# A second gradient accumulator, third buffers for YT and h_in, a warm SiLU, SEL cleared by GpSimd, and a new step order

## The chip, the cores and the metric

The kernel runs on one core of a Trainium2 chip. A core has five engines that each take their instructions in order: PE (TensorE, the matrix array), DVE (VectorE), ACT (ScalarE), POOL (GpSimd) and SP (SyncE, which here only issues DMAs). They meet through semaphores. SBUF is the on-chip memory (128 partitions), PSUM the accumulators that PE writes, DRAM what lies outside. The metric is the device time of one execution in microseconds; the median of three runs before the change is 574.38 us (573.65 to 574.65).

## The reference

One block of a network, forward and backward: layer norm, then a state-space convolution (S4) times a gate that is the SiLU of a two-layer feed-forward net, plus the input. The kernel returns the output and the gradients of eleven inputs.

```python
def _fwd_reference(A_u, ..., B_w1, B_w2):          # L = 2048 rows, D = 512, N = 128 states, F = 1792
    def _A_ref(u, A_re, A_im, B_re, B_im, C_re, C_im, log_dt, Dskip):
        dt = jnp.exp(log_dt)[:, None]
        P = jnp.exp((dt * (A_re + 1j * A_im))[:, :, None] * l[None, None, :])
        K = jnp.einsum("dn,dnl,dn->dl", Cc, P, dt * Bc).real        # the convolution kernel
        ...                                                         # causal convolution of u with K, by FFT
        return y + u * Dskip
    def _B_ref(x, w1, w2):
        return einsum(_silu(einsum(x, w1)), w2)
    xn = _layernorm(A_u)
    return A_u + _A_ref(xn, ...) * _silu(_B_ref(xn, B_w1, B_w2))

def reference(...):
    _out, _vjp = jax.vjp(_f, A_u, A_A_re, ..., B_w1, B_w2)
    return (_out, *_vjp(grad_out))
```

## The kernel before

The work is cut into some thirty streams. Each stream is a Python generator that emits a few instructions and yields; one such piece is a step. Nothing reorders the steps at run time: the string `PLAN`, cut by `/` into seven stages, names one stream per letter, and `play` takes the next step of that stream. So the string fixes the order of instructions on every engine and every queue. Two more strings go with it. `WAYS` says for each copy out of PSUM (through `k.ev`, line 113 or 114) whether ACT (`A`) or DVE (`D`) does it. `SLOTS` says which buffer each tile takes.

The stages, with the streams that matter below:

- Stage 0, the start. `1` loads the rows of x (SP) and log_dt (ACT queue); `0` loads the weights W1 and W2 (SP); `p` loads the S4 parameters by transposing DMAs (SP, line 363); `2` and `3` make constants and masks, `SEL` among them (lines 242 to 263, DVE and POOL); `4` makes the FFT tables `TF` with Sin on ACT (line 281); `5` makes smaller tables, with Sin at lines 314 and 315; `6` is the layer norm (statistics at line 375 and `xn` at 383 on DVE, the power `rstd` at 379 on POOL); `7` takes Exp of log_dt (506), forms `lamr` (508, DVE) and then 31 exponentials `mag_all` (511, ACT); `J` transposes rows of xn into XT on PE; `F` is the feed-forward net: `ps_h` on PE (755), a copy to `hT`, SiLU into `aT` (763), a store of hT to DRAM (765), then `ps_o` (772).
- Stage 1 and 2. `P`, `Q` and `R` build the convolution kernel on DVE, ACT and PE (`ps_k`, line 643), with round trips through DRAM (`ds<-Md`, `Ed`, `Yd`, `Kb`); `X` and `C` are the FFTs of input and kernel and their product; `F` goes on.
- Stage 3. The backward convolutions (`B`, `D`), and the backward feed-forward products `A` (1160) and `x` (1184).
- Stages 4 and 5. The gradients of the S4 parameters in four blocks of 128 channels: `N` folds the kernel gradient, `Y` loads the turned powers YT for sixteen groups (transposing DMAs, line 986; every fourth group is loaded plain as Yn and turned on PE), `V` multiplies (`ps_v`, 1012), `T` forms products on DVE (1029 to 1033), `S` sums them on PE (`psS`, 1049), and `Z` ends each block (lines 1067 to 1119). Beside them run the weight gradients: `h` loads rows of h (`h_in`, 1203), `t` turns them and takes SiLU (`a_tok`), `w` multiplies (1223); `g` loads `dh_tok` by transposing DMAs (1238) and `v` multiplies (1252).
- Stage 6. The rest of `v` and `w`, and the backward layer norm `i`, `k`, `m`.

A step of `Z` in one block: several DVE products; the accumulator `g_acc` is written at line 1094 and added to at 1099 and 1100; `gout` is written at 1089 and 1098; PE transposes `gout` (`pt_g`, 1104), ACT copies it back, POOL stores it in six DMAs (1111); PE reduces `g_acc` over the partitions (`pd`, 1114), DVE writes the result into the first row of `g_acc` (1117), and POOL stores that (1119). Before the change `g_acc` and `gout` have one buffer each.

Of the kernel before, what the change touches and what calls it, by code (L numbers as in the profile page):

```python
# [18 lines left out]
P = 128  # L19
# [26 lines left out]
""".replace("\n", "").split("/")


SLOTS = dict(x.split("=") for x in """
fp.XT=01010101;pf.pf=012010021021021021021010120120120120120120120120120210210210201201201202102102102021021021021021201  # L50
201201201201021012102102102102102102020120210210202102102021021201201212102102102102102102010101201201202010202102120102
0120120120120210210210201;fp.hT=0101010101010101;fp.ob=0101010;dft.w8=21301203120132032103213032013021;pc.pc=01010110101
010010101010010101010101010101010101010101010101010101010010101010101010101010110101010101010101010101010101010101010101
010101010101010101010101010101010101001011010101010101010101010101010101010101010101010101011110101010101010110010101010
101010101010101;tbl.tv=01011101110101011101001011101010;tbl.ts=01010101010111010010101000101101;tbl.W=010101101011010110
10;dft.t4=010100101010;gate.g=01237456;gate.S=01;da.doT=01010101;dftb.w8b=1010;da.dhT8=20120120;go.go_s=01010101;da.dhT6
=10101010;go.go_r=010101;go.go_g=01010101;da.pd_s=101010101010;go.go_x=01201201;sb.YT=0101010101010101;sb.Eb=10101010;sb
.Gb=01010101;sb.Vb=1010101010101010;sb.Tp=0101010101010101;sb.Sa=0101;fw.h_in=01010101010101;fw.a_tok=01010101010101;fw.
o11=01201201201201;fw.dh_tok=2012012;fw.o10=0101010;lw.pd_l=012301;lw.Gt=20132013;lw.m=010101;lw.o1=12031203
""".replace("\n", "").split(";") if x)  # L60

WAYS = """J=DAADADAA;
F=AAADAAAAADDADAAAAAAAAAAAAAAAAAAAAAAAAAAADAAAADDAAAAAAAAADDDADAAAADDDDAAA;
X=AAAAAAAAAAAAAAAAAAAAAAAAAAAAAAAA;
U=AD;
R=DDAADAAAAAAAAAAAAAADAAAADADDDAAAAAAAADDAAAAAAAAA;
C=DDDAAAAAAAAAAAAAAAAADDAAAAAAAADAAAAAADADDAADADAAADADDDADAAAAAAAA;
W=DDDDDDDDDDDDDD;  # L70
D=AAAADDAAAAAAAAADAAADAAAAAADAAAAAAADAAAAA;
d=DDDDDAAA;
B=AAAAAAAAAAAAAADAAAAAAAAAAAAAAADAAAAADADAAAAAADAAAAAADAAD;
x=AAADDAADAAAA;
V=AAADADAADAADAAAADDDAAAAAAAAAAAAAAAADADAAAAAAAAAAAAAAAAAAAAAAAAAA;
Y=DAAAADAA;
w=AAADAAAAADAAAD;
v=AADDADADAAAAAAADDAAAAAAAAAAA"""


class Placed:
# [79 lines left out]
def setup_tiles(k, wp):  # L161

    D = k.D
    t = SimpleNamespace()
    def new(nm, shape, dt=F32, pool=wp):
        setattr(t, nm, pool.tile([P] + shape, dt, name=nm))
    for nm in ("ldt", "Ar", "Ai"):
        new(nm, [D], BF16)
    new("lamr", [D])
    new("ph", [D])  # L170
    new("MS", [4, 128], BF16)
    new("il", [16], I32)
# [17 lines left out]
    new("m4", [4])  # L190
    new("rl", [NE])
# [45 lines left out]
def gen_masks(k, w):  # L237

    nc, const = k.nc, k.const
    G = nc.gpsimd  # L240
    MS, FO, SEL = w.MS, k.FO, k.SEL
    nc.vector.memset(MS[:], 0.0)
    nc.vector.memset(FO[:], 0.0)
    nc.vector.memset(SEL[:], 0.0)
    yield
    I = k.ident
    par = lambda t: t.rearrange("p (r b a) -> p r b a", b=2, a=4)
# [19 lines left out]
def gen_tables(k, w):  # L267
# [4 lines left out]
    def twiddles(h):  # L272
# [8 lines left out]
        nc.scalar.activation(out=k.TF[:, hs], in_=low, func=ACT.Sin, scale=-2 * PI_LO / 2.0 ** PB)  # L281
        yield
    yield from twiddles(0)
# [775 lines left out]
def gen_ssm_grads(k, b, sb):  # L1059
# [408 lines left out]
```

## Time and profile before

The profiled execution took 573.83 us, of which 572.1 us lie between its first and last instruction (the span). All times below are counted from the start of the span.

| | busy us | share of the span |
|---|---|---|
| PE | 528.9 | 92% |
| DVE | 526.4 | 92% |
| ACT | 446.4 | 78% |
| POOL | 75.6 | 13% |
| mean granted TensorE clock | 0.984 | |

An instruction's row gives its start, its length, engine, line, operation and tiles (`out<-in`); in brackets stands how long its engine was idle before it and what it waited for. "PEq", "SPq" and so on are an engine's queue work: issuing DMAs, semaphores. A window row gives the busy time of each engine in a stretch, then the clock that the throttle granted to PE (1.00 is full speed) and the share of time in which the DMA engines were busy. The chain of waits is the chain of work that ended last, followed back from the end; it shows by how much each instruction pushes the next (its pitch), a little less than its length where two overlap.

### The profile page before, as it was taken

What the parts mean: (1) busy time and instruction counts of PE and PEld (TensorE: products, weight loads), DVE (VectorE), ACT (ScalarE), POOL (GpSimd) and SP (SyncE); (2) the same over time, 40 slices, a digit from 0 to 9 for tenths busy, and PEclk for the clock granted to TensorE, in tenths of its full rate; (3) what the DMA queues carried; (4) which work ended last, traced back from release to release, by engine and by line L of the source; (5) the groups of instructions that cost most, each with busy time, mean ns of one, the idle gap of its engine ahead of it and who ended that gap; (6) DMA issues with size and microseconds to landing.
All of it is one profiled execution on the core that took longest, in us unless ns stands there. A gap on an engine that the chain in (4) does not pass through costs nothing.

```text
span 572.1 us, 14533 instructions
## 1 busy us (share of the span) xinstructions
PE 528.9 (92%) x6008; PEld 395.0 (69%) x6008; DVE 526.4 (92%) x826; ACT 446.4 (78%) x553; POOL 75.6 (13%) x163
## 2 busy tenths in 40 slices
PE   0599998999898999999999999999999999989995
PEld 0366766686767685877686766777668797857674
DVE  8999999999999879999999899969999999977994
ACT  7989989999999859998888785674477676843662
POOL 5321101010100011000000000000000030324121
PEclk9879999999999999999999999999999999989998
DMA  9988897988989989878888979898999989989893
GB/s 236 319 307 173 252 283 227 341 254 227 306 260 261 299 292 337 286 258 237 288 282 276 301 234 299 231 222 190 278 222 231 203 254 198 270 161 221 244 229 131
DMA packets 156643, 144.75 MB, mean 253 GB/s; under 512 B 83488, under 2 KB 132896, under 8 KB 153504
## 3 DMA queue, kind: packets, MB, share of 16 engines
q1 hardware_dynamic: 146816, 121.00, 78.6%
q0 software_dynamic: 6640, 19.67, 10.2%
q10 hardware_dynamic: 3120, 3.15, 1.7%
q8 instruction: 47, 0.77, 0.6%
q14 instruction: 20, 0.16, 0.1%
HBM read 62.91 MB, written 59.38 MB: 214 GB/s over the span
## 4 chain that ended last, share of the span: by engine, by line
PE 58%; DVE 22%; DMA 9%; ACT 4%; SPq 3%; issue 3%; POOL 1%; DVEq 0%; ACTq 0%; POOLq 0%
PE ps_w L1252 7%; PE ps_da L1160 7%; PE ps_dx L1184 7%; PE ps_w L1223 6%; PE ps_o L772 4%; PE pt_t L135 4%; PE ps_i L444 3%; PE ps_i L457 3%; PE ps_h L755 3%; DMA ds<-Md 2%; PE ps_s L399 2%; PE ps_s L427 2%; PE pt_f L413 2%; PE psS L1049 2%; DVE ds L602 2%
## 5 line engine op out<-in xcount | busy, mean ns | idle before, releaser
L113 ACT CAST dA<-ps_s 128x1024 bf16<-128x1024 f32 x86 | 86.2, 1032 | 5.7 <-PE ps_s L399 3.7
L755 PE MATMUL ps_h<-XT,W 128*128 128x256 bf16 x448 | 61.1, 289 | 11.9 <-DVE XT L114 6.3
L755 PEld LDWEIGHTS <-W 128*128 128x128 bf16 x448 | 44.6, 103 | 21.3 <-issue 11.5
L113 ACT CAST Vb<-ps_v 128x672 bf16<-128x672 f32 x55 | 39.0, 731 | 24.5 <-PE ps_v L1012 13.1
L1160 PE MATMUL ps_da<-doT,W 128*128 128x256 bf16 x448 | 56.3, 273 | 0.0
L1252 PE MATMUL ps_w<-dh_tok,xn 128*128 128x256 bf16 x448 | 52.3, 273 | 0.0
L1223 PE MATMUL ps_w<-YD,a_tok 128*128 128x512 bf16 x224 | 52.3, 388 | 0.0
L113 ACT CAST dB<-ps_i 128x1024 bf16<-128x1024 f32 x40 | 40.9, 1044 | 14.2 <-PE ps_i L444 13.9
L772 PE MATMUL ps_o<-W,aT 128*128 128x512 bf16 x224 | 51.0, 379 | 0.1
L1184 PE MATMUL ps_dx<-W,dhT 128*128 128x512 bf16 x224 | 50.9, 379 | 0.0
L1160 PEld LDWEIGHTS <-W 128*128 128x128 bf16 x448 | 41.5, 98 | 8.2 <-issue 1.8
L1252 PEld LDWEIGHTS <-xn 128*128 128x128 bf16 x448 | 43.0, 98 | 5.6 <-issue 0.6
L1163 DVE TENSOR_TENSOR dhT<-ps_da,dhT 128x512 bf16<-128x512 f32 x56 | 37.8, 683 | 6.1 <-PE ps_da L1160 4.6
L1223 PEld LDWEIGHTS <-a_tok 128*128 128x128 bf16 x224 | 22.0, 100 | 24.5 <-issue 2.2
L772 PEld LDWEIGHTS <-aT 128*128 128x128 bf16 x224 | 21.0, 98 | 25.1 <-issue 1.2
L1184 PEld LDWEIGHTS <-dhT 128*128 128x128 bf16 x224 | 21.1, 98 | 24.8 <-issue 1.6
L1214 ACT ACTIVATE a_tok<-pt_t 128x1024 bf16<-128x1024 bf16 x28 | 28.7, 1036 | 4.6 <-PE pt_t L135 4.4
L574 ACT ACTIVATE sn<-V 128x2048 bf16<-128x2048 int16 (+1 forms) x16 | 30.4, 1899 | 0.2
L113 ACT CAST o<-ps_w 128x256 bf16<-128x256 f32 (+1 forms) x33 | 14.6, 451 | 19.6 <-PE ps_w L1252 13.1
L470 DVE TENSOR_TENSOR cm<-sp_in,dA 128x2048 bf16<-128x2048 bf16 x24 | 29.3, 1219 | 0.7
L472 DVE TENSOR_TENSOR sp_in<-sp_in,dA 128x2048 bf16<-128x2048 bf16 x24 | 29.3, 1220 | 0.6
L643 PE MATMUL ps_k<-W,YD 128*128 128x84 bf16 x512 | 25.2, 201 | 4.7 <-DVE ds L114 1.4
(239 smaller groups left out, 1246.0 us busy)
## 6 DMA issues: line engine op xcount, KB each, us to landing
Yd<-YD SPq DMA_DIRECT2D x8, 1024.0 KB, 5.2
sp_in<-Ud SPq DMA_DIRECT2D x8, 1024.0 KB, 9.1
h_in<-Hd SPq DMA_DIRECT2D x14, 512.0 KB, 5.6
Ed<-ds SPq DMA_DIRECT2D x8, 672.0 KB, 5.2
Eb<-Ed SPq DMA_DIRECT2D x8, 672.0 KB, 5.2
Hd<-hT POOLq DMA_DIRECT2D x8, 512.0 KB, 7.2
Ud<-dA SPq DMA_DIRECT2D x8, 512.0 KB, 6.4
KXd<-dA SPq DMA_DIRECT2D x4, 1024.0 KB, 5.6
```

The lines of the kernel that those rows point to most:

```text
L113: return self.nc.scalar.copy(out=out, in_=in_)
L470: TT(out=t2[:], in0=b[:, :, gs], in1=a[:, 1:2, gs].to_broadcast([P, 2, n, P]), op=ALU.mult)
L472: TT(out=b[:, :, gs], in0=b[:, :, gs], in1=a[:, 0:1, gs].to_broadcast([P, 2, n, P]), op=ALU.mult)
L574: nc.scalar.activation(out=sn[:, 0:n], in_=low, func=ACT.Sin, scale=-2 * PI_LO / 2.0 ** PB)
L755: nc.tensor.matmul(out=ps[:, j], lhsT=k.W1[:, dk, ft * P:ft * P + P], rhs=XTv[:, :, dk, :], start=(dk == 0), stop=(dk == DK - 1))
L772: nc.tensor.matmul(out=ps[:], lhsT=aT[:, ft, t * P:t * P + P], rhs=k.W2[:, ft, :], start=(ft == 0), stop=(ft == FT - 1))
L1160: nc.tensor.matmul(out=ps[:, j], lhsT=k.W2[:, ft, dk * P:dk * P + P], rhs=dTv[:, :, dk, :], start=(dk == 0), stop=(dk == DK - 1))
L1163: nc.vector.tensor_tensor(out=dh[:, i0:i0 + 2, :], in0=ps[:], in1=dh[:, i0:i0 + 2, :], op=ALU.mult)
L1184: nc.tensor.matmul(out=ps[:], lhsT=dhs[ft // 8][:, ft % 8, t * P:t * P + P], rhs=k.W1[:, :, ft * P:ft * P + P], start=(ft == 0), stop=(ft ...
L1214: yield from turned(k, lambda t: h[:, t], k.T, a, lambda out, in_: k.nc.scalar.activation(out=out, in_=in_, func=ACT.Silu))
L1223: nc.tensor.matmul(out=ps[:], lhsT=at[:, t, :], rhs=k.do[:, t, :], start=(t == 0), stop=(t == k.T - 1))
L1252: nc.tensor.matmul(out=ps[:], lhsT=k.xn[:, t, dk * P:dk * P + P], rhs=dh[:, t].rearrange("p j n -> p (j n)"), start=(t == 0), stop=(t == k ...
```

## The change

In the code, five places:

```diff
@@ gen_masks
     nc.vector.memset(MS[:], 0.0)
     nc.vector.memset(FO[:], 0.0)
-    nc.vector.memset(SEL[:], 0.0)
     yield
...
     G.tensor_copy(out=par(MS[:, 3])[:, :, 1], in_=par(MS[:, 1])[:, :, 1])
     yield
+    G.memset(SEL[:], 0.0)
+    yield
     for a in range(4):
         G.tensor_copy(out=lane(SEL[:, :, a])[:, :, :, a], in_=lane(MS[:])[:, :, :, a])
@@ gen_tables
         low = prod[:].bitcast(I16).rearrange("p t c (k w) -> p t c k w", w=2)[:, :, :, :, 0]
+        if h == 0:
+            nc.scalar.activation(out=w.warm[:], in_=k.onesf[:], func=ACT.Silu)
         nc.scalar.activation(out=k.TF[:, hs], in_=low, func=ACT.Sin, scale=-2 * PI_LO / 2.0 ** PB)
@@ gen_ssm_loads
-        YT = sb.tile([P, 2, 8, P], BF16, name="YT", tag="YT", bufs=2)
+        YT = sb.tile([P, 2, 8, P], BF16, name="YT", tag="YT", bufs=3)
@@ gen_ssm_grads
-    acc = tmp("acc", 1)
+    acc = sb.tile([P, 1, P], F32, name="g_acc", tag="g_acc", bufs=2)
@@ gen_dw2_loads
-        h = fw.tile([P, k.T, P], BF16, name="h_in", tag="h_in", bufs=2)
+        h = fw.tile([P, k.T, P], BF16, name="h_in", tag="h_in", bufs=3)
```

`warm` is a new tile of one element; nothing reads it. `PLAN`, `SLOTS` and `WAYS` are written anew. The first stage of `PLAN`:

```diff
-3212215p557536266767177p177667560077417767p73730757676J7J6F77077p7668475F73666676J778653601F773787F487F3J6F7FF74648FF5F6
-FFF6377F866JF7688F767476F8/
+221p32551512p5566073777171165553766767777J767774J6376777pF6767703076767884p6J7677777707F6067FJF86F46673F5F743FF776646FF6
+78F7366F883F7867F8FF86364/
```

Read letter by letter, this changes the order in the first stage as follows.

- SP issued x rows 0-1, Ar, x 2-3, Ai, x 4-7, W1 (two parts), x 8-11, Br, Bi, W1 (last part), W2, Cr, Ci, W2, x 12-15. It now issues Ar, x 0-1, x 2-3, Ai, W1 (first part), the other three x loads, Br, Bi, W1 (two parts), Cr, Ci, W2 (two parts).
- ACT took Exp of dt, the two Sin of lines 314 and 315, 23 exponentials, one copy of `ps_h`, the other eight exponentials, a copy of `ps_h`, Sin of TF's first half, a copy of XT, a copy of `ps_h`, SiLU, three copies, SiLU, Sin of TF's second half. It now takes the two Sin of lines 314 and 315, Exp of dt, all 31 exponentials, copies of `ps_h`, XT and `ps_h`, the warm SiLU, Sin of TF's first half, a copy, SiLU, three copies, SiLU, Sin of TF's second half.
- DVE makes the first small tables and the first product with the Sin tables (317) ahead of the first statistics, and `lamr` right behind the first two of them.
- On POOL the memset of SEL comes between the second and the third `rstd`.
- The PSUM slots of the first transposes and `ps_h` were 0,1,2,0,1,0,0,2,1; they are 0,1,2,0,1,2,0,2,1.

In the later stages every stream's own sequence is kept, and the letters are interleaved a little differently. Where the prediction touches them:

- `WAYS`: in stages 0 to 2, six copies of `ps_k` and three of `ps_h` go from DVE to ACT; three small copies into `KE`, and five of `ps_h` or `ps_o`, go from ACT to DVE; the FFT's exchange two each way. In stages 3 to 6 DVE hands some six copies more to ACT.
- `SLOTS`: YT rotates 2,0,1 instead of 0,1; h_in 0,1,2 instead of 0,1; g_acc 0,1,0,1.
- Block 2 of `Z`: DVE ran, from line 1117 of block 1 on, the product Tq of group 13, the first pair of `Z`, the group's difference Ts, then four steps of `Z` to the accumulator, Tp of group 14, and the last step. Now it runs 1117, Tq, Ts, four steps of `Z`, Tp, the accumulator's step, Tq of group 14, the last step. PE runs between `pd` of block 1 and the transpose of block 2: two transposes of h, psS 12, two `ps_v`, psS 13, a group of 1252, `ps_v`, a transpose of Yn, a group of 1252, two `ps_v`, a group of 1252, `ps_v`.
- SP in stage 5: the transposing loads of `dh_tok` for the third pair of row blocks stood ahead of Eb 12 and behind Yn of group 15; both now stand behind that Yn. h rows 12 are loaded in stage 5 instead of 6.

More of the change, by code (lines that the diff above doesn't have):

```diff
@@ new lines @@
+78F7366F883F7867F8FF86364/QXJFXPFFFJFPXFXXFX9XFXPFFPFXPPFFFFFFFFXUPFFQFJFFQRQQUQPFXQFXXQXPFQQXXRPQJPFRFPRFFPFXXFFRRFQFRF
+FFXXRRFFPFQXQQQRXFQXFUFFQRQRXJQXFFQRPRRQRXXRPRRQPRFFPFRRFXXFPUJRPRFFRQFPQRRXRQRRRQRQXFXFRQQCFQRXFXXQRRFXRPXFFFQRPFPPRQFP
+RCUCCCFCCFRRCCQRCFCRQCRFCXQQFCQFQXPCQQFXFQPCRCCQFFCFCCPRRFQXPRFFRXFRXFCCCRRFRXXXCFFFFQQQCRFRCQCFXRPQRCFRXQPCFCQRQRCQCRFQ
+CCQCRRRFRPFCXCPRRJFXXRXXPRFRXPUFFXCRJXRPPCRXQFCCXPXQFQQFQCCFFRCFCCQCQRQPFCFCFFQFQFFCRFQRFCFFCRJRCCCPCCRRCCFCRCRCCRCQCPRC
+QXQCFPXXXQFPRQCCRXXFCJFCCXQXRPCQRRQCRFFCQRQXFQCRFRXFRRFRPXXRPRFCXFRPCXFRRRFFFCXCXFCXFQRQRFFCCCCFRUCFJQCCCCRFFQQFQCRQCQCQ
@@ new lines @@
+RCRRCRCCRRCRRCRRRUCCCRQCRRRCRRRFCCCCRCJFCC/FCGFCFGGGGGCCCFCFFCFCGCGFCCCCCFFGCGFFMCFCCCGFGCFFGCGHCCGCGHCGHFWCCFCFGCCFGGCG
+CGCCGCFGCFCCFCCWCCWCWHWCWHHHCCWGDCLWWDCGHWWWCCCWDWWDCWDWWDDWWDGWWMWWDDDLDLMLWLDWMDMWDDDDD/DdDasEddDWadDEoDAsBAAAoABaDoAB
+AAAADoBADDBBAoBDBAoABDAAABDBsDAAAABBBADaADBBAABoBBBADDBBDBBlEBxBBDosABBAABOBABxaBEOBDxOolxoDlOABBxBdBBABODdDaOBxBOxsDOBo
+OODxoxBDoaoxBDlOBBAsBOABxBBOoADaaABDABBBOBDDBBABBABABDdABDEAAAdABBBBAAABosdoADODoABOBAdBOABoxDDABBABABOEoDABDBlOADDxsDDB
+AoxOADDOBoABxoDBAOABDsAoBBxODBdAxOAOBDABBAaaDBAAdBlDAoOBADAODBxxABOBDBxDDBDoBxBBBoxsoBxBDAEBBDOBBoABAsAaOAOxDABBxODxsBBa
@@ new lines @@
+BBBoxAABBBEABxsBBBOxBBABaABBAOOAOABBAaBAABBBBxBAABAAABddAxBBBBBBBAABBBBxABBABBA/ANNNYAANYNYNxVAxVsaVVdAxAYVVxdVVAVTAYYVA
+ATxVTVVYsxAAVVAAAxTsAVVTTVNASNTNxASAVTANVATAVVAVVAAVTNAYTVTxTYYTxTxYSYTTVAxTVYVSVVVVVVS/hTthVtTtYtVYVtVTtVtVStTVVThTwTVV
+TVSVVVTTwVTYwYYtVTtwSgVVVVSwTwtTTVtgYZYVwYTNZVVNTvSVhZTTYSNTYNVVvYVTgVvthVvVwVvVvSTtVtTVTVtVVZZYvVYSZTTVYwVSgtTVtZTwTZVt
+TVTVwVtSVTTTVVVSVTTTTwTwVvVVVvZNYZvTVZZNYVZNvNvZYYhthTvNttYtSVtvVZtwTtTZvTSZYYSVtwTTVhVYvSVVVVTVVZwYVwVVTtTwVYTtYhSVtvTV
+TTVwSVVtVTVVSSTVYYTTTVgVZwVVZTTZwwYgwTVZYvTVTttTZtYSVTSgVhTVSvZZVVZVvYYvwZZgtTvZTVVVZSTvVTVVTZTZVwZVvtTSvwwSTTZThtTTttZv
@@ L46 @@
+ZStSZhgttZZZvZZgvtvwwtgZZtwZwvvZvZZvhwv/itikhvkivvttkvkikvwvmtkvmwkvkkwmktmgktkivmvwkmktwmkgvwvikvvmmkkvmtkvvkktkmivvtkw
+mwgmkvkmikmwmkkkmmwkvmvkvvkvvvmvmvvmvvmm
 """.replace("\n", "").split("/")
 SLOTS = dict(x.split("=") for x in """
[L50 to L52 removed]
@@ L58 @@
-.Gb=01010101;sb.Vb=1010101010101010;sb.Tp=0101010101010101;sb.Sa=0101;fw.h_in=01010101010101;fw.a_tok=01010101010101;fw.
-o11=01201201201201;fw.dh_tok=2012012;fw.o10=0101010;lw.pd_l=012301;lw.Gt=20132013;lw.m=010101;lw.o1=12031203
+fp.XT=01010101;pf.pf=012012021021201212012021012012010120120120120120120120120120102102102101201201201012012012012012102
+102102102102012012012012012102101201212012012012012012012102102102102120120120120120121020121210101012010120120210210210
+2102012012102102020121021;fp.hT=0101010101010101;dft.w8=21301203121030230123012320312031;pc.pc=0101010101010001010101010
@@ new lines @@
+101010101010101010101010101010101001010101010101010101010101010101010101010101010101010101010101101010101010101010101010
+101010101010101010101010101010110101010101010101010101010101010101010101010101001010101010101010101010101010101010101010
+1;fp.ob=0101010;tbl.tv=01011101110101011010110101010101;tbl.ts=01010101010111010010101000101101;tbl.W=010101101011010110
+10;dft.t4=010011010101;gate.g=10237456;gate.S=01;da.doT=01010101;da.dhT8=20120120;dftb.w8b=1010;da.dhT6=10101010;go.go_s
+=01010101;go.go_r=010101;go.go_g=01010101;go.go_x=01201201;da.pd_s=010101010101;sb.YT=2012012012012012;sb.Eb=01010101;sb
@@ L60 @@
+.Gb=01010101;sb.Vb=0101010101010101;sb.Tp=0101010101010101;sb.Sa=1010;fw.h_in=01201201201201;fw.a_tok=10101010101010;fw.
+o11=01201201201201;sb.g_acc=0101;fw.dh_tok=0120120;fw.o10=1010101;lw.pd_l=012301;lw.Gt=01230123;lw.m=010101;lw.o1=120312
+03
 """.replace("\n", "").split(";") if x)
 WAYS = """J=DAADADAA;
-F=AAADAAAAADDADAAAAAAAAAAAAAAAAAAAAAAAAAAADAAAADDAAAAAAAAADDDADAAAADDDDAAA;
+F=AAADAAAAADADDAAAADADAAAAAAAAAAAAAAAAAAAAAAADADDAAAAAAAAADDDADAAADADDDAAA;
 X=AAAAAAAAAAAAAAAAAAAAAAAAAAAAAAAA;
@@ L67 @@
 U=AD;
-R=DDAADAAAAAAAAAAAAAADAAAADADDDAAAAAAAADDAAAAAAAAA;
-C=DDDAAAAAAAAAAAAAAAAADDAAAAAAAADAAAAAADADDAADADAAADADDDADAAAAAAAA;
+R=AAAAAAAAAAAAAAAAAAADAADDDAADAAAAAADAADAAAAAAAAAA;
+C=DDDAAAAAAAAAAAAAAAAADDAAAAAAAADAAAAAADAADAADDAADADADDDADAAAAAAAA;
 W=DDDDDDDDDDDDDD;
[L71 to L77, printed above, removed]
@@ L78 @@
-v=AADDADADAAAAAAADDAAAAAAAAAAA"""
+D=AAAADDAAAAAAAAADAAAAAADAAADAAAAAAADAAADA;
+d=DDAADAAA;
+B=AAAAAAAAAAAAAADAAAAAAAAAAAAAAAAAAAAAAADAAAADAAAAAAAADADA;
+x=AADAAAADADAA;
+V=DAADADDADAAAADAADDAAAAAAAAAAAAAAAAADAAAAAAAAAAAAAAAAAAAAAAAAAAAA;
+Y=AADDDAAA;
+w=AADAAAAAAADAAA;
+v=DAADAAAAAAADAAAAAAAAAAAAAAAA"""
 class Placed:
@@ L190, in setup_tiles @@
     new("m4", [4])
+    new("warm", [1])
     new("rl", [NE])
```

22 lines of the change are left out of this document (removed).

## The prediction

> **What bounds the kernel now.** I read first the windows by stage, then the waits, then the two places where TensorE (PE) stands still, instruction by instruction. The windows (columns: stretch, length, busy of PE, weight load, DVE, ACT, POOL, granted clock, DMA share, GB/s):
>
> ```profile
> 45.00:255.00 210.00, 198.77 (x2532) 150.47 (x2529) 199.75 (x260) 195.12 (x224) 20.59 (x28) 1.00 0.89 272
> 255.00:375.00 120.00, 119.65 (x1500) 86.97 (x1500) 112.52 (x146) 95.20 (x100) 6.48 (x12) 1.00 0.87 269
> 375.00:435.00 60.00, 58.20 (x564) 41.86 (x562) 54.81 (x81) 35.84 (x46) 1.10 (x2) 1.00 1.02 221
> 435.00:495.00 60.00, 60.00 (x674) 48.38 (x672) 58.55 (x94) 42.73 (x69) 11.61 (x21) 1.00 1.05 228
> 495.00:513.00 18.00, 15.38 (x151) 11.43 (x149) 14.33 (x29) 9.78 (x18) 3.74 (x7) 0.91 0.98 222
> 513.00:566.00 53.00, 52.57 (x444) 38.99 (x442) 45.73 (x116) 27.28 (x45) 14.80 (x26) 1.00 0.87 219
> ```
>
> From 45 us on PE is the rope: 119.65 of 120, 60.00 of 60 and 52.57 of 53 leave nothing to win there, since no matmul is added or removed. Time can come only from where PE is idle or slow: the start (before 45), 11.2 us of gaps in 45 to 255 where DVE (95%) and ACT (93%) are full too, 1.8 us in 375 to 435, and 2.6 us in 495 to 513. The last is one hole. DVE, POOL and PE around it (start, us, instruction, idle before it and its releaser):
>
> ```profile
> 492.30 0.27 DVE L1117 TENSOR_TENSOR g_acc<-pd,dt 1x128 bf16<-1x128 f32 x1
> ...
> 497.77 0.68 DVE L1089 TENSOR_TENSOR gout<-g_t,dt 128x512 bf16<-128x512 f32 x1
> ...
> 502.82 0.29 DVE L1094 TENSOR_TENSOR g_acc<-g_u 128x128 f32<-128x128 f32 x1 [3.49 <-DMA out_dram<-g_acc]
> ```
>
> ```profile
> 489.60 3.18 POOL L1111 DMA_DIRECT2D out_dram<-gout  x6 [10.73 <-ACT gout L1108]
> ...
> 494.06 0.52 POOL L1119 DMA_DIRECT2D out_dram<-g_acc  x1
> ```
>
> ```profile
> 504.81 0.51 PE L1104 MATMUL pt_g<-ident,gout 128*128 128x128 bf16 x6 [2.62 <-DVE gout L1098]
> ...
> 506.18 5.30 PE L1223 MATMUL ps_w<-YD,a_tok 128*128 128x512 bf16 x16
> ```
>
> An undisturbed group of the same sixteen matmuls, and the window behind the hole (granted clock third from the end):
>
> ```profile
> 454.35 3.62 PE L1223 MATMUL ps_w<-YD,a_tok 128*128 128x512 bf16 x16
> ```
>
> ```profile
> 506.00:508.00 2.00, 2.00 (x12) 0.88 (x9) 1.97 (x4) 2.00 (x5) 0.95 (x2) 0.54 0.46 72
> ```
>
> The single accumulator of block 1 is stored by a DMA issued at 494.06, behind six stores of `gout` on POOL's queue. Block 2 wants the same buffer at 499.3; DVE stands 3.49 us until the store has landed, and PE, whose next instruction needs DVE's `gout`, stands 2.62 us. Then the granted clock falls to 0.54, and the sixteen matmuls of L1223 take 5.30 us, where the group at 454.35 takes 3.62. So the hole costs 2.62 + 1.68 = 4.30 us.
>
> **Part 1: two accumulators.** Blocks 0 to 3 alternate, so block 2 takes the buffer of block 0, long stored. The 3.49 us go; what is late next? First, DVE's own work. Between the store's source (L1117) and the `gout` that PE needs the new order has one product more (Tq of the next group, 0.77); at the pitches of the chain of waits that stretch sums to 9.5 us. PE's work from the `pd` matmul ahead of L1117 to that transpose is 11.0 us in the new order: three groups of L1252 (1.75 each), two sums psS (1.17), three transposes (0.45), six short ps_v (0.29) and `pd`. DVE stands some 1.1 us behind PE there, so the two meet within half a microsecond. Second, `gout` has one buffer still:
>
> ```profile
> DMA to landing us min/median/max: 2.2/4.0/7.2
> ```
>
> Its last store was issued by 492.78 and lands, by this row, between 495.0 and 500.0, while block 2 writes `gout` at 497.77 without a wait. At the slow end that would be a new wait of 2.2 us. I take 0.4 us lost to both, so -3.9 us; bounds -1.0 (the `gout` store lands last, and the clock falls again) and -4.3.
>
> [...]
>
> **Part 2: the start.** ACT's first instructions, and its two lines with the later table loads (xcount: ns min/median/max, first and last start):
>
> ```profile
> 4.28 0.63 ACT L506 ACTIVATE dt<-ldt 128x512 bf16<-128x512 bf16 x1 [1.33 <-DMA ldt<-in_A_log_dt_dram]
> 4.93 1.28 ACT L314 ACT_TABLE_LOAD   x1
> 6.22 0.40 ACT L314 ACTIVATE sf<-kf,mpi 128x128 f32<-128x128 int32 x1
> 6.53 0.44 ACT L315 ACTIVATE sv<-kq,mpi 128x192 f32<-128x192 int32 x1
> 6.99 1.28 ACT L511 ACT_TABLE_LOAD   x1
> 8.28 12.06 ACT L511 ACTIVATE mag_all<-lamr 128x512 bf16<-128x512 f32 x23
> ```
>
> ```profile
> L281 ACT ACTIVATE TF<-prod x2: 1893/1902/1910, 26.8 to 36.6; 128x2048 bf16<-128x2048 int16 x2
> L281 ACT ACT_TABLE_LOAD  x1: 1283/1283/1283, 25.5 to 25.5; - x1
> ```
>
> ```profile
> 30.07 1.28 ACT L763 ACT_TABLE_LOAD   x1
> ```
>
> DVE, POOL, SP and PE in the same stretch, and the window of the low clock:
>
> ```profile
> 1.57 0.91 DVE L244 MEMSET SEL<- 128x1024 uint32 x1 [0.16 <-issue]
> ...
> 4.77 0.69 DVE L375 BATCH_NORM_STATS2 st<-x_sb 128x6 f32<-128x512 bf16 x1
> ```
>
> ```profile
> 17.96 1.39 POOL L379 TENSOR_TENSOR rstd<-ve,mhalf 128x4 f32<-128x4 f32 x1 [4.50 <-DVE ve L378]
> ```
>
> ```profile
> 1.20 1.24 SPq L363 DMA_TRANSPOSE Ar<-in_A_A_re_dram  x1
> ```
>
> ```profile
> 29.29 5.28 PE L755 MATMUL ps_h<-XT,W 128*128 128x256 bf16 x24 [1.93 <-DVE hT L114]
> 34.36 0.98 PE L135 MATMUL pt_t<-ident,xn 128*128 128x128 bf16 x8
> 35.18 3.18 PE L772 MATMUL ps_o<-W,aT 128*128 128x512 bf16 x14
> ```
>
> ```profile
> 25.00:35.00 10.00, 7.57 (x38) 5.37 (x38) 9.86 (x24) 9.57 (x10) 4.88 (x7) 0.50 0.93 351
> ```
>
> ACT is the full engine here: 23 of the 31 exponentials follow each other from 8.28 to 20.3, the other eight behind one evacuation. The second Sin of L281, at 36.6, has no load ahead of it although SiLU ran in between: SiLU's table holds Sin. With a one-element SiLU ahead of the first L281, the two loads at 25.5 and 30.07 become one: -1.28. The warm activation costs between nothing and the 0.40 of `sf`, 128 times its size; I take 0.3. The new order also puts Sin of L314 before Exp of dt, so of the three loads before 8.28 one goes, but nothing comes of it: the 31 exponentials wait for `lamr`, and DVE comes to `lamr` later. The SEL memset leaves DVE (-0.91), but Ar's transpose now stands first on SP and takes 1.24 us, so x arrives 1.2 to 1.3 us later, and the statistics that began at 4.77 begin near 5.7. Net zero to -0.3, and rstd of the first rows 1.7 us late, which the full ACT hides. On POOL the memset lies ahead of the third `rstd`; I price it at 0.91 (DVE's own row, with 4 bytes an element) to 1.82 (two bytes), and POOL has waited 4.50 us by then. Without that cover it would delay four rows of xn by as much.
>
> What PE gains is the clock. It is at half rate from 25 to 35 us, because it gets work only in pieces (7.57 of these 10 us, the last wait 1.93). In the new order all exponentials go before the first evacuation (16.3 us for 31 at the pitch of the 23, so near 24.6), then evacuations follow at short intervals, and the PSUM slots rotate 0,1,2,0,1,2: PE should run on from about 25.2 instead of 29.3, so the clock should come back some 3 us earlier, and the second SiLU, ahead of the second table Sin, ends near 35.3. The first output matmuls can then start near 34 instead of 35.18. I take -1.5 us; bounds -3.0 (clock and table in full) and +2.0 (late x passed on to PE, as the 1.7 us of rstd).
>
> **Part 3: evacuations and order, 45 to 255 us.** DVE loses six copies of `ps_k` and takes three small KE ones, and takes two more of `ps_h` or `ps_o`:
>
> ```profile
> 133.90 0.50 DVE L114 CAST ds<-ps_k 128x336 bf16<-128x336 f32 x1
> ```
>
> 6 x 0.50 less 3 x 0.25 (half a `ps_k` row) less 2 x 0.75 (by 512 elements against 336) is 0.75 us off DVE in 210. The rest is the same list in another order. I take -0.5; bounds -5.6 and +5.6, half of the 11.2 us of PE gaps either way, since nothing in the trace prices an order.
>
> **Part 4: third YT and h_in.**
>
> ```profile
> SPq L986 <- PE ps_v L1012: 7.3, 5, 2.5
> ```
>
> SP, which issues in order, stood 7.3 us for a free YT and no longer does. But PE has only 1.8 us of gaps in 375 to 435, and the DMA share is 1.02 to 1.05 there, so earlier issues only queue elsewhere. The moved transposes of `dh_tok` (both of the third pair now behind Yn of group 15) sum to the same SP time. -0.4; bounds -1.8 (all of the idle in 375 to 435) and +1.0 (an earlier h_in ahead of a needed YT, half a YT issue of the 2.5 us that one wait took). Evacuations moved off DVE after 255 lie under a full PE: zero; without that cover, some six of 0.7 us, the size of `ps_k` to YT copies. The last two stages' new step order: zero, PE is gapless to 565.6.
>
> **The sum.** -1.5 - 0.5 - 0.4 - 3.9 = -6.3 us. The profiled execution took 573.83 (span 572.1), 0.55 under the median of 574.38; so 567.5 there and 568.1 by the median. I say 568.0.
>
> **The rivals.** (a) *The wait only moves*: `gout`'s store takes the accumulator's place, the clock falls again; part 1 gives -1.0 and the total is 571. For it: same queue, same landing rows. Against it: `gout` of block 2 was written at 497.77 with no wait.
> (b) *The new order loses in the full stretch*: between 45 and 255 PE's gaps grow from 11.2 us because three full engines wait for each other in other places; DVE at 95% has nothing to catch up with. It decides from +5.8 us of gaps on (17 instead of 11.2). At seven tenths more (+8) the kernel takes 576.6, slower. For it: each step of the 600 was moved a little, and one wait of 2 us on DVE there would pass on in full. Against it: DVE and ACT both get lighter, and the sequence of SP is nearly the same.
> (c) *More comes*: the start's bound of -3.0 and 3 us of gaps saved, 564.
> (d) *The table count does not fall* (the warm SiLU gets a load of its own and the Sin another): the start gives 0, the total 569.5; this lies in the forecast's own range.
> (e) *The hole costs only its idle time*: had the low clock behind it another cause, which stays, the total would be 569.8. Against it: of the six stages quoted from 45 us on, only the one with the hole is under 1.00. [...]
>
> **How the numbers follow.** Forecast with (d) 0.61, own range 565 to 571; (a) 0.12; (b) 0.16; (c) 0.08; (e) 0.03. About 0.2% (1.15 us) is what a measurement can tell from no change. Faster takes the forecast, (a), (c) and (e), 0.84, less the 0.06 in which part 2's upper bound and a tenth more gaps in the middle meet them: 0.78; same 0.06; slower 0.16, which is (b). The range 563.5 to 575.0 leaves out most of (b) and the far end of (c).
>
> **What would show it.** Right: no DVE wait on `out_dram<-g_acc`; PE's clock 1.00 throughout 495 to 513 and 17.5 or more of 18 busy; one load fewer between the exponentials and the first SiLU of `aT`, five in all instead of seven; clock back before 33 us. Wrong: a DVE wait on `out_dram<-gout`; PE below 198 in the 210 us of the middle; the clock at half anywhere after 40 us.

## The result, and the profile after

The changed kernel takes 576.2 us (median of 22 runs, 573.29 to 580.0), the kernel before 572.67 in the runs beside it (22 runs, 568.89 to 576.54). The ratio is 1.0062, with a 95% interval of 1.0039 to 1.0084: the change costs 3.5 us. The prediction was 568.0, range 563.5 to 575.0, on the other side. The profiled execution of the changed kernel took 574.64 (span 572.9), that of before 573.83 (span 572.1): these two lie only 0.8 apart, so a part of the 3.5 us shows in other executions than these.

The windows of the changed kernel that answer to those of before (same columns):

```profile
45.00:255.00 210.00, 199.43 (x2530) 151.51 (x2528) 198.93 (x254) 194.97 (x223) 22.64 (x28) 0.99 0.89 274
255.00:375.00 120.00, 119.38 (x1493) 86.32 (x1490) 111.97 (x145) 97.33 (x103) 6.47 (x12) 1.00 0.86 263
375.00:435.00 60.00, 58.24 (x568) 42.26 (x566) 54.51 (x79) 35.12 (x45) 1.10 (x2) 1.00 1.05 221
435.00:495.00 60.00, 59.20 (x664) 47.29 (x662) 57.93 (x92) 43.45 (x68) 11.18 (x21) 1.00 1.02 233
495.00:513.00 18.00, 17.96 (x202) 14.83 (x200) 17.83 (x37) 11.00 (x20) 5.20 (x10) 1.00 1.14 256
513.00:566.00 53.00, 50.16 (x420) 37.15 (x417) 42.19 (x109) 28.68 (x48) 13.76 (x25) 1.00 0.84 206
```

The hole is gone: PE is busy 17.96 of 18 us at full clock (before 15.38 at 0.91), and DVE writes the accumulator of block 2 without a wait (timeline of DVE):

```profile
493.69 0.27 DVE L1122 TENSOR_TENSOR g_acc<-pd,dt 1x128 bf16<-1x128 f32 x1
...
501.53 0.28 DVE L1099 TENSOR_TENSOR g_acc<-g_u 128x128 f32<-128x128 f32 x1
```

In the last window PE has 2.4 us less left to do than before (50.16 against 52.57): it is done early. Yet the span is no shorter. What ends it stands in the timelines of POOL, first after, then before:

```profile
565.51 0.54 POOL L1322 DMA_DIRECT2D out_dram<-o  x1 [1.58 <-DVE o L1320]
```

```profile
564.69 0.54 POOL L1317 DMA_DIRECT2D out_dram<-o  x1 [1.04 <-DVE o L1315]
```

This is the last store of `out_1`, the end of the backward layer norm on DVE. The span ends 7.4 us behind it in both (572.9 and 572.1), and 7.3 to 7.4 behind it in each of the 17 profiles of this study, while its distance from the end of PE's last matmul runs from 5.0 us (e3 below) to 9.7 (the changed kernel). The chain of waits of the kernel before ends all the same on PE and on ACT's last copy, at 565.60; that the layer norm sets the end there too is read from the constant distance, not from that chain. After the change the chain runs through the layer norm. It started late. DVE after, and then before, at that place:

```profile
526.04 0.28 DVE L1122 TENSOR_TENSOR g_acc<-pd,dt 1x128 bf16<-1x128 f32 x1 [5.72 <-PE pd L1119]
526.25 0.67 DVE L115 CAST o<-ps_w 128x512 bf16<-128x512 f32 x1
529.73 0.69 DVE L1298 SCALAR_TENSOR_TENSOR pd_l<-pd_l,ds 128x512 bf16<-128x512 bf16 x1 [2.81 <-DMA out_dram<-gout]
```

```profile
526.26 0.28 DVE L1117 TENSOR_TENSOR g_acc<-pd,dt 1x128 bf16<-1x128 f32 x1 [2.08 <-PE pd L1114]
526.47 0.67 DVE L1293 SCALAR_TENSOR_TENSOR pd_l<-pd_l,ds 128x512 bf16<-128x512 bf16 x1
```

Two waits have grown. `pd` of the last block now stands on PE behind a group of L1228 and one of L1257, so DVE waits 5.72 us for it instead of 2.08. And the first instruction of the layer norm waits 2.81 us more, on a store of `gout` with which it has nothing to do. SP has the same trouble with the fourth `Gt`; its rows name no releaser, so the row of its waits between 515 and 535 us (sum, times, longest) stands below them:

```profile
520.44 0.67 SPq L1277 DMA_DIRECT2D pd_l<-Pd  x1
529.72 0.33 SPq L1279 DMA_DIRECT2D Gt<-in_grad_out_dram  x1
```

```profile
SPq L1279 <- DMA out_dram<-gout: 8.0, 2, 6.3
```

The reason is where the tiles lie. The pools `sb` and, later, `lw` end at the same address, so distances down from it, worked out from the tiles' sizes in bytes per partition, show what lies on what:

```
                      before            after
g_acc                 0 to 512          0 to 1024 (two)
g_u2,g_u1,g_t2,g_t1   512 to 6656       1024 to 7168
gout                  6656 to 8192      7168 to 8704
lw: o1 (4 x 2048)     0 to 8192         0 to 8192
lw: m (2 x 32)        8192 to 8256      8192 to 8256
lw: Gt, last buffer   8256 to 10304     8256 to 10304
```

Before, `gout` lay wholly under the first buffer of `o1`, which the layer norm comes to only with its third group of rows (`lw.o1=1203...`). The second accumulator's 512 bytes push it under `m`, which the first instruction of the layer norm writes (its accumulated sum), and under `Gt`. So both wait until the stores of `gout`, issued from 521.37 on, have landed.

### The profile page after: what moved, and what is told of

It reads as the page before. It is cut to its first block, busy times and chain, and to the rows that moved or that the text cites. A ratio compares the mean times of both kernels' runs of the same rounds, so it can differ in the third digit from the quotient of the medians.

```text
span 572.9 us, 14534 instructions
## 1 busy us (share of the span) xinstructions
PE 526.5 (92%) x6008; PEld 394.0 (69%) x6008; DVE 524.7 (92%) x818; ACT 448.1 (78%) x559; POOL 78.3 (14%) x164
## 4 chain that ended last, share of the span: by engine, by line
PE 38%; DVE 31%; issue 10%; DMA 8%; ACT 6%; POOL 3%; SPq 2%; ACTq 0%; POOLq 0%; DVEq 0%
PE ps_da L1165 7%; PE ps_dx L1189 6%; PE ps_i L449 4%; PE ps_i L462 3%; DMA ds<-Md 3%; PE ps_o L777 3%; PE pt_t L136 2%; PE ps_s L432 2%; DVE Tq L1034 2%; DVE ds L607 2%; PE ps_w L1228 2%; DVE Tp L1034 2%; PE ps_s L404 2%; DMA out_dram<-gout 2%; DVE Tp L1038 2%
## 5 line engine op out<-in xcount | busy, mean ns | idle before, releaser
L760 PE MATMUL ps_h<-XT,W 128*128 128x256 bf16 x448 | 59.5, 283 | 11.0 <-ACT hT L114 6.6
L1257 PE MATMUL ps_w<-dh_tok,xn 128*128 128x256 bf16 x448 | 52.4, 273 | 0.0
L1228 PE MATMUL ps_w<-YD,a_tok 128*128 128x512 bf16 x224 | 50.6, 379 | 0.0
L1257 PEld LDWEIGHTS <-xn 128*128 128x128 bf16 x448 | 43.0, 98 | 5.7 <-issue 0.4
L1228 PEld LDWEIGHTS <-a_tok 128*128 128x128 bf16 x224 | 21.6, 98 | 23.2 <-ACT a_tok L1219 0.2
L114 ACT CAST o<-ps_w 128x256 bf16<-128x256 f32 (+1 forms) x37 | 16.2, 442 | 21.4 <-PE ps_w L1257 10.3
L449 PE MATMUL ps_i<-I,sp_in 64*128 64x128 bf16 x768 | 27.6, 217 | 2.1 <-ACT dB L114 1.1
```

What stands on the lines that cost most here:

```text
L114: return self.nc.scalar.copy(out=out, in_=in_)
L449: nc.tensor.matmul(out=ps[:, z, g], lhsT=Y[zs, c, g0 + g, :], rhs=k.I2[zs, c].rearrange("p c m -> p (c m)"), start=(c == 0), stop=(c == 1))
L760: nc.tensor.matmul(out=ps[:, j], lhsT=k.W1[:, dk, ft * P:ft * P + P], rhs=XTv[:, :, dk, :], start=(dk == 0), stop=(dk == DK - 1))
L1228: nc.tensor.matmul(out=ps[:], lhsT=at[:, t, :], rhs=k.do[:, t, :], start=(t == 0), stop=(t == k.T - 1))
L1257: nc.tensor.matmul(out=ps[:], lhsT=k.xn[:, t, dk * P:dk * P + P], rhs=dh[:, t].rearrange("p j n -> p (j n)"), start=(t == 0), stop=(t == k ...
```

## The experiments

Ratios are to the kernel before, with 95% intervals; its median in the runs beside them was 572.35 (e1 to e4), 573.26 (e5 to e8), 573.54 (e9 to e12) and 572.77 (e13 to e15). The ratios differ a little from the quotients of the medians (e5: 0.9991 against 0.9976); a difference of 1 us or less is not to be read from either. Each kernel has one profile.

**The end.** First the edit of e1, in the changed kernel; e2 adds an order of the last letters of the plan's sixth part, in which `pd` goes ahead of the group of L1228, and gives that group's evacuation to ACT:

```diff
         o1 = lw.tile([P, 2, k.D], BF16, name="o1", tag="o1", bufs=4)
+        if c == 0:
+            lw.tile([P, 1, P], F32, name="gap")
```

```diff
-...wwtgZZtwZwvvZvZZvhwv/      w=AADAAAAAAADAAA
+...wwtgZZtwZvZZwvZvvhwv/      w=AADAAAAAAAAAAA
```

> The changed kernel with 512 bytes left free at the top of the last pool, so that Gt's fourth buffer and m no longer lie on gout (o1's first buffer lies there, as in the kernel before). Theory A (the end has two ropes, PE and the backward layer norm on DVE, and the second accumulator's 512 bytes put gout under buffers that the layer norm needs first): the 2.81 us DVE wait on out_dram<-gout goes, the layer norm begins near 527 instead of 529.7, its last store is issued near 562.7 instead of 565.5, and then PE's last store (issued near 565.1, 5.9 us before the end) sets the end: about 1.9 us less than the changed kernel, 574.3 against 576.2. Theory B (the loss lies in the new order before 495 us, and the end follows PE as the prediction had it): the wait goes too, but the time stays within 0.6 us of 576.2.

> The changed kernel with the same 512 bytes free, and with the last pd matmul one group of 1.75 us behind the transposes of gout instead of behind 5.2 us of weight gradients; the evacuation of the weight gradient that comes after it goes to ACT. Theory A: DVE's 5.72 us wait for pd shrinks to about 2, the layer norm begins near 523 and is done near 559, well ahead of PE. Then PE alone sets the end, so nothing more is won over the kernel with the free bytes alone: within 0.7 us of it, some 574 us. If the layer norm is the only rope, 3.5 us more are won (570.5). Theory B: 576 as well.

e1: 574.05, ratio 1.0046 (1.0021 to 1.0071). e2: 574.09, 1.0025 (0.9993 to 1.0058). In both the wait on `gout` is gone; in e2 that for `pd` has shrunk too. The first DVE rows of the end, e1 and e2:

```profile
527.92 0.28 DVE L1122 TENSOR_TENSOR g_acc<-pd,dt 1x128 bf16<-1x128 f32 x1 [5.72 <-PE pd L1119]
...
528.72 0.67 DVE L1298 SCALAR_TENSOR_TENSOR pd_l<-pd_l,ds 128x512 bf16<-128x512 bf16 x1
```

```profile
525.04 0.28 DVE L1105 TENSOR_TENSOR g_acc<-pd,dt 1x128 bf16<-1x128 f32 x1 [2.27 <-PE pd L1102]
525.25 0.67 DVE L1281 SCALAR_TENSOR_TENSOR pd_l<-pd_l,ds 128x512 bf16<-128x512 bf16 x1
...
537.22 0.69 DVE L1305 TENSOR_TENSOR o<-o,pd_l 128x1024 bf16<-128x1024 bf16 x1 [4.99 <-ACT pd_l L1288]
```

By the medians the free bytes bring 2.1 us, as theory A said (574.3); by the ratios 0.9, with intervals that meet, so that theory B is not ruled out by the times. The profile shows less of it than theory A: in e1 `pd` itself comes 1.9 us later than in the changed kernel, and the last store of the layer norm is issued at 564.84, not at 562.7. The earlier `pd` brings nothing more, as theory A said for e2, but not because the layer norm is done early: in e2 it starts 3.5 us earlier than in e1 and then waits 4.99 us for ACT, whose copy of PE's results stands ahead of the work that DVE needs and waits 5.24 us for PE. Here PE is the rope again, through ACT.

The same pieces in the kernel before, e3 with the two buffers (and `sb.g_acc=0101` in the slots), e4 with the free bytes as well:

```diff
-    acc = tmp("acc", 1)
+    acc = sb.tile([P, 1, P], F32, name="g_acc", tag="g_acc", bufs=2)
+            lw.tile([P, 1, P], F32, name="gap")
```

> The kernel before with two buffers for the accumulator and nothing else. The prediction's reading (PE is the only rope): the hole of 4.3 us goes, 3.5 to 4 us less than the kernel before, 569. Theory A: the second buffer moves gout by 512 bytes under Gt and m, the layer norm has to wait until gout's last store of block 3 has landed (issued up to 528 in the kernel before, some 3.5 earlier here, landing 2.2 to 7.2 us later), so DVE begins it near 529 instead of 526.5 and ends 2 to 3 us later than before, although PE is done 4 us earlier: time from 0 to 3 us over the kernel before, 573 to 576, with a DVE wait on out_dram<-gout of 3 us or more ahead of the layer norm.

> The kernel before with two buffers for the accumulator and 512 bytes free in the last pool, so that the layer norm's first buffers keep clear of gout. Theory A: no wait on gout, the layer norm begins near 523 and PE's hole is gone, so both ropes are 3.5 to 4 us shorter: 568.7 to 569.2. Theory B and the prediction's reading: the same, 569. If the hole was worth only its idle time: 570.

e3: 580.39, ratio 1.0141 (1.0099 to 1.0183). e4: 571.25, 0.9992 (0.9964 to 1.0021). The last windows of e3 and its DVE row, then the windows of e4:

```profile
495.00:513.00 18.00, 17.95 (x207) 15.04 (x207) 16.19 (x34) 11.21 (x21) 5.12 (x10) 1.00 1.07 220
513.00:566.00 53.00, 44.76 (x334) 31.29 (x337) 40.73 (x107) 22.83 (x36) 11.83 (x21) 0.90 0.88 203
```

```profile
530.93 0.69 DVE L1293 SCALAR_TENSOR_TENSOR pd_l<-pd_l,ds 128x512 bf16<-128x512 bf16 x1 [8.78 <-DMA out_dram<-gout]
```

```profile
495.00:513.00 18.00, 17.95 (x207) 15.07 (x207) 16.62 (x34) 10.66 (x20) 5.58 (x10) 1.00 1.04 237
513.00:566.00 53.00, 47.25 (x376) 34.45 (x379) 42.68 (x109) 25.71 (x42) 12.98 (x23) 0.99 0.86 217
```

With nothing but the second buffer, DVE stands 8.78 us, PE loses 8.2 of 53 us and its clock, and the kernel is 8 us slower, where theory A had 0 to 3; 512 unused bytes take all of that back. This is the clearest of the runs: the new wait is shown, and its cause is the place of `gout`. Why it costs so much more here than in the changed kernel stands in PE's row of e3: a copy of PE's result (`o`) is queued on DVE behind the instruction that waits, and PE stands until that copy is made. In the changed kernel the copy goes ahead of that instruction (the row at 526.25 above), and PE has no such wait.

```profile
534.10 3.57 PE L1252 MATMUL ps_w<-dh_tok,xn 128*128 128x256 bf16 x16 [7.78 <-DVE o L114]
```

But e4 was to win 4 us, and it wins 1.1 by its median and 0.5 by its ratio, within the interval.

**Why the hole is worth less.** Theory D, stated with e5 below, says that the hole differs between executions, with the time at which the accumulator's store lands. Five kernels below (e5, e6, e7, e9, e10) have one accumulator and this stretch as before. DVE's wait for it and PE's window, first of one in which PE does not stand (e5), then of the dearest (e10):

```profile
499.20 0.29 DVE L1097 TENSOR_TENSOR g_acc<-g_u 128x128 f32<-128x128 f32 x1 [0.85 <-DMA out_dram<-g_acc]
```

```profile
495.00:513.00 18.00, 18.00 (x207) 14.97 (x205) 15.89 (x32) 10.80 (x20) 5.50 (x10) 1.00 1.04 229
```

```profile
504.64 0.29 DVE L1109 TENSOR_TENSOR g_acc<-g_u 128x128 f32<-128x128 f32 x1 [3.23 <-DMA out_dram<-g_acc]
```

```profile
495.00:513.00 18.00, 15.41 (x154) 12.73 (x153) 14.60 (x31) 11.00 (x19) 5.40 (x10) 0.91 0.91 201
```

All six of that kind, from the same two rows of each:

```
                     before   e5     e6     e7     e9     e10
DVE waits, us         3.49   0.85   2.78   0.63   3.44   3.23
PE busy of 18 us     15.38  18.00  16.43  18.00  15.51  15.41
granted clock         0.91   1.00   1.00   1.00   1.00   0.91
```

PE's idle time in the six is 2.62, 0, 1.57, 0, 2.49 and 2.59 us, 1.55 in the mean, and the clock falls in two of them only. With the 1.68 of the prediction for each of these two the hole costs 1.55 + 2 x 1.68 / 6 = 2.1 us on average, not 4.30. D holds as to the spread. Of its sign, a wait under 2.5 us instead of 3.49, e5 and e7 are for it, e6 lies between, and e9 and e10, with more than 3 us, are against it: the profile of before was a dear one, but not a rare one. The six are different kernels with one profile each, so a difference between kernels is not told apart from one between executions. The times agree better with 2.1 than with 4.30: with the free bytes, two accumulators bring 0.5 us in e4 against before (interval from 2.1 won to 1.2 lost), and 2.6 in e12 below against e5, give or take some 2.4.

**Start, middle and later stages.** The plan, slots and engine choices have seven parts, one for each stage; these kernels take each part from before (b) or after (a). Steps that one order has issued earlier than the other were moved across the seam. The code lines of the diff go with the stage.

```
stage          0 1 2 3 4 5 6
e6             a b b b b b b    start
e7             a a a b b b b    start and middle (to 255 us)
e8             b b b a a a a    later stages, with the 512 free bytes
e9             b a a b b b b    middle
e11            a b b a a a a    start and later stages, with the free bytes
```

e5 is the kernel before with the two lines of the warm SiLU:

```diff
+        if h == 0:
+            nc.scalar.activation(out=w.warm[:], in_=k.onesf[:], func=ACT.Silu)
```

> The kernel before with the one-element SiLU ahead of the first table Sin and nothing else. Table loads fall from seven to six (SiLU's own goes), 1.28 us less on ACT less 0.2 for the one element. If ACT sets the pace of the start, as the prediction took it, 0.5 to 1 us less than the kernel before; if not, within 0.4 us of it. The hole at 495 to 513 is untouched. Theory D (the hole's size hangs on when the accumulator's store lands, and that differs from execution to execution; the profiled execution of before, 8.66 us from issue to use, was a dear one): DVE's wait on out_dram<-g_acc in this new profile is under 2.5 us, not 3.49. Against D: it is 3 us or more again.

> The kernel before with the whole start of the changed one (its first stage's order, warm SiLU, selection table cleared by GpSimd), the rest in the order of before, one accumulator. The prediction's part 2: 1.5 us less (570.9). Theory C (the changed kernel's later executions stand 1.7 us behind before from 60 us on, the start lost): 1 to 1.5 us more than before, 573.6, with PE's busy time in 30 to 45 near 12.5 to 13 instead of 15 and half-clock records behind 40 us. Theory D on the hole as for the kernel with the warm SiLU.

> The kernel before with the changed kernel's first three stages (start, and the order and evacuations up to about 255 us) and before's later stages with one accumulator. Prediction (parts 2 and 3): 2.0 us less, 570.4. Theory C: the same instructions stand 2 to 2.5 us later than in before at 255 us, and the time is 574.5 to 575. The share of the middle is this less the kernel with the start alone; the rival (b) of the prediction wants 5.8 us or more of it, theory C about 1. Theory D on the hole as above.

> The complement: before's first three stages, then the changed kernel's later ones (third YT and h_in, two accumulators, its order and evacuations), with 512 bytes left free so that the layer norm keeps clear of gout. Prediction (parts 1 and 4): 4.3 us less, 568.1. Theory A with D: the hole is gone, the third buffers and order lose 0.7 to 1.1 us before 495, PE sets the end: 1 us less than before, 571.3, near the 571.25 of the kernel with two accumulators and the free bytes alone.

> The kernel before with only the changed kernel's second and third stages (order, evacuations and PSUM slots from about 43 to 255 us); start, later stages, accumulator and buffers as before. Theory E (the order of the middle costs by itself): 1.5 to 2.5 us more than the kernel before, with the same instructions 1.5 to 2.5 us later at 255 us. Rival F (the middle's order is no worse, but it starts from rows that the new start brings late, so only the two together lose): within 0.7 us of before.

> The changed kernel with before's order, evacuations and slots in the second and third stage, and 512 bytes free in the last pool. Theory E: all that is left of the change is the start (nothing), the accumulator (1 to 2 us won) and the later order (nothing): 1 to 2 us less than before, as the kernel with only the later stages changed, and 2 to 3 us less than the changed kernel with the free bytes. Rival F: the same, since the two no longer meet. If the start loses by itself: about the time of before.

Measured: e5 571.88, ratio 0.9991 (0.9956 to 1.0025); e6 573.19, 1.0017 (0.9977 to 1.0056); e7 575.27, 1.0039 (1.0000 to 1.0078); e8 571.26, 0.9981 (0.9949 to 1.0012); e9 573.24, 1.0001 (0.9979 to 1.0023); e11 571.91, 0.9977 (0.9954 to 0.9999). None of e5, e6, e8 and e9 is clear of no change: the start wins nothing that can be told (the warm SiLU alone perhaps half a microsecond), the later stages win about 1 us, near what e4 wins, and the middle alone costs nothing. But with the new start under it the middle does cost: e1, which is e11 with the new middle, stands at 1.0046 against 0.9977, some 4 us more, with intervals that do not meet (e2, at 1.0025, 3 more). On the later stages of before the same step, e7 against e6, is only 1.3 us, with intervals that overlap. Theory C's time for e7, 574.5 to 575, is near what came, and its 1 to 1.5 us for e6 cannot be told from nothing. Theory E falls by e9, F stands.

Two guesses at the reason. e10 gives the kernel before the new choice of engines for the evacuations of stages 0 to 2, and nothing else. e13 is e1 with the last rows of the normalised input ahead of the last six steps of the SSM weights on DVE; e14 is e1 with before's choice of engines; e15 has both.

```diff
 e13, end of the plan's first part
-...678F7366F883F7867F8FF86364/
+...67F7366F3F767FFF6364888888/
```

> The kernel before with the changed kernel's choice of engine for the evacuations of the streams J, F, X, U, R and C (R gives three of its ten DVE copies to ACT, F takes two more to DVE), its order untouched. The prediction's part 3 took 0.5 us less for this. Theory E wants the order to blame, so within 0.7 us of before. If ACT (195 of 210 us busy) pays for what DVE is spared, 0.7 to 2 us more.

> The changed kernel with the 512 free bytes, and the six last steps of the SSM weights (sp_t and CT, 4.8 us on DVE) moved behind the last four rows of the normalised input at the end of the first stage. Theory G (late rows): xn of the last rows begins near 38.8 instead of 41.3, PE's waits of 1.05 and 0.28 us on xn go, PE is busy 14 us or more in 30 to 45 instead of 12.5 to 12.9, no half clock before 60 us, and the time is 1 to 2 us less than with the free bytes alone: 572 to 573. Theory H (choice of engines): within 0.7 us of 574.

> The changed kernel with the 512 free bytes and before's choice of engine for the evacuations of J, F, X, U, R and C, in the changed order. Theory H: 2 to 2.5 us less than with the free bytes alone, 571.5 to 572. Theory G: within 0.7 us of 574; the order was made for its own choice of engines, so it may also lose up to 2 us.

> Both edits in the changed kernel with the 512 free bytes. If G alone is right, as the kernel with the early rows; if H alone, as the one with before's engines; if each is half of it, 570.5 to 571.5.

e10: 576.32, 1.0042 (1.0016 to 1.0068). e13: 575.65, 1.0050 (1.0020 to 1.0081). e14: 586.52, 1.0263 (1.0225 to 1.0301). e15: 588.49, 1.0281 (1.0239 to 1.0322). Order and choice of engine belong together: either choice in the other's order loses, 2.4 us one way and 12 the other, so H falls. In e13 the rows do come early (xn at 38.33 instead of 41.31 in e1), and PE is busy 14.16 of 15 us in 30 to 45 (e1: 12.89). The gap only moves on; windows of e13 and PE's next waits:

```profile
30.00:45.00 15.00, 14.16 (x113) 9.41 (x111) 13.56 (x27) 13.10 (x15) 6.24 (x12) 0.95 0.78 276
45.00:60.00 15.00, 11.55 (x73) 7.77 (x73) 14.86 (x24) 10.94 (x10) 1.73 (x2) 0.77 0.70 178
```

```profile
47.08 1.03 PE L775 MATMUL ps_h<-XT,W 128*128 128x256 bf16 x8 [2.69 <-DVE hT L130]
49.46 2.93 PE L775 MATMUL ps_h<-XT,W 128*128 128x256 bf16 x13 [1.35 <-DVE hT L130]
```

DVE is full there (14.86 of 15) and PE waits for its copies to `hT`; that the steps moved behind the rows are what makes these late is likely, but no run shows it. So G falls as well; why the new middle costs only on the new start stays open.

**A version that beats both.** e12 is the kernel before with the warm SiLU, two accumulators and the 512 free bytes (the diffs of e5 and e4).

> The kernel before with the three small pieces that looked useful: the one-element SiLU, two accumulators, 512 bytes free in the last pool. If the pieces add up (0.5 to 1 from the table load that goes, 1 to 2 from the hole): 1.5 to 3 us less than before. PE then has no gap over 2 us between 435 and 560, and the layer norm no wait on gout.

569.73 (568.64 to 572.87), ratio 0.9946 (0.9924 to 0.9969): by the ratios 3.1 us faster than before and some 6.5 than the changed kernel, and clear of no change. Its pieces alone, e5 and e4, had 0.5 us each, within their intervals; how the 3.1 divide between them is not shown. PE is busy 17.95 of 18 us at full clock in 495 to 513, and the layer norm starts without a wait on `gout` (window and DVE row of e12):

```profile
495.00:513.00 18.00, 17.95 (x207) 15.01 (x206) 16.22 (x32) 10.94 (x21) 5.38 (x10) 1.00 1.03 233
```

```profile
521.82 0.67 DVE L1296 SCALAR_TENSOR_TENSOR pd_l<-pd_l,ds 128x512 bf16<-128x512 bf16 x1
```

## Why the prediction was wrong

- *"From 45 us on PE is the rope"*: the step that failed in its mechanism. At the end there are two ropes, PE and DVE's layer norm, and the span ends 7.3 to 7.4 us behind the last store of the second, in the kernel before too. In the profiles PE was done 2.4 us earlier after the change (its last matmuls take 7.15 us from 556.01, to 563.16; before from 558.42, to 565.57), the layer norm 0.8 later. *"The last two stages' new step order: zero, PE is gapless"* looked at PE alone and missed 3.6 us of longer waiting for `pd` and 2.81 for `gout`.
- *Part 1, what is late next*: DVE's own work and the single `gout` were named, and at block 2 neither was late. Rival (a), the wait that moves to `gout`'s store, did happen, but at block 3 and on other tiles; the step did not ask what the second buffer's 512 bytes push where. Right in mechanism: no wait on `out_dram<-g_acc`, full clock, 17.96 busy.
- *Part 1, the size*: 4.30 was that of one execution. Six profiles give 2.1 on average, and e4 wins 0.5 where the term was -3.9.
- *"Then the granted clock falls to 0.54"*: that is one execution, and the fall does not come with every such hole. Behind 2.62 us of idle ahead of the transposes the granted clock was 0.54 (before, 506 to 508), behind 2.37 it was 0.52 (e10, 508 to 510), and behind 2.43 it was 1.00 (e9, throughout 500 to 510); so the idle time alone does not decide it. PE's rows of e10 and e9:

```profile
506.63 0.82 PE L1119 MATMUL pt_g<-ident,gout 128*128 128x128 bf16 x6 [2.37 <-DVE gout L1113]
```

```profile
505.92 0.51 PE L1119 MATMUL pt_g<-ident,gout 128*128 128x128 bf16 x6 [2.43 <-DVE gout L1113]
```

- *Part 2*: five table loads, as predicted (at 3.59, 5.65, 26.75, 242.02 and 413.98), but the start's gain is not 1.5 us: e6 stands at 1.0017, which cannot be told from 0. PE's clock did come back earlier (1.00 in 30 to 45 against 0.83), and PE then had gaps, 12.46 busy of 15 against 15.00. Work in pieces, the reason given for the half clock, was the author's reading, and no run shows it: before the change PE was busy 5.75 of the 10 us from 15 on, at a granted 0.99 and behind 6.32 us of idle, and 7.57 of the next 10, at 0.50 and behind 3.31. Eight matmuls of L755 took 1.87 us at 16.12, 1.86 at 25.49 and 1.04 at 42.57: by their length PE was no faster at 16.12 than at 25.49.
- *Part 3*: by its size the term that missed most. -0.5 was 0 by itself (e9) and some +4 on the new start (e1 against e11). The prediction summed start and middle as if each were worth the same with and without the other, and it said itself that nothing in the trace prices an order; why the two together lose stays open. Rival (b), the order that loses, is nearest to what came. That its 576.6 lies near the measured 576.2 is luck, since the mix of reasons is another: its point of decision, 5.8 us of gaps, was set against a gain that was not there, and the sign named for it (PE under 198 in 45 to 255) did not come: 199.43.
- *Part 4*: -0.4 is within what e8 and e4 can tell (0.9981 and 0.9992).

Step by step by the ratios: the new start and later stages with the free bytes -1.3 us (e11), the new middle on top of them +4.0 (e1 against e11), the wait on `gout` +0.9 (changed kernel against e1), together +3.6. That this meets the measured +3.5 proves nothing, since each step starts where the last one ends. The single terms are known less well: the wait on `gout` is 0.9 by ratios and 2.1 by medians, and the middle is 1.3 when it is taken from e7 and e6.

## What to carry to other kernels

A buffer added to one pool moves everything below it (here `gout`, by 512 bytes): look what the next pool lays over each tile that a slow store still reads. Follow the last store back on each engine before calling one of them the bound; an engine at 99% (here PE, 52.57 of 53 us) need not set the end. A stall that hangs on a DMA landing should be priced from several profiles, not from the one at hand. And two changes of order have to be tried together as well as one by one: here neither start nor middle cost anything by itself that could be told.

## What was not expected of the hardware

The same 256-byte store of the accumulator lands at very different times: from its issue to DVE's start behind it, 494.06 to 502.82, 8.8 us in the kernel before, and 493.21 to 499.20, 6.0 us in e5, whose program differs only by the warm SiLU at the start. Why is not shown. DVE wants the buffer 5.0 to 5.3 us behind the issue in all six kernels of the table, so the spread alone decides between a hole and none.
